# Two residue pairs at once in the last, single-batch filter group

## The chip, the cores and the metric

The kernel runs on one core of a Trainium2 chip. The metric is the device time of one execution in microseconds, the median over several runs. Five engines run their own instruction streams: TensorE (PE in the profile, with its weight loads as PEld), VectorE (DVE), ScalarE (ACT), GpSimd (POOL) and SyncE (SP), whose stream issues most of the DMA transfers.

## The reference

Two blocks follow each other for 8 batches of a 3008 x 256 array. The first filters along the sequence by a real FFT, a product with a complex filter and the inverse FFT; the second is an MLP mixer, first over the tokens, then over the channels.

```python
X = np.fft.rfft(x, axis=1)                       # x: (8, 3008, 256)
y = np.fft.irfft(X * (filt_r + 1j * filt_i), n=3008, axis=1)
h = np.maximum(y.transpose(0, 2, 1) @ w_tok1, 0.0) @ w_tok2     # 3008 -> 256 -> 3008
u = y + h.transpose(0, 2, 1)
out = u + np.maximum(u @ w_ch1, 0.0) @ w_ch2                    # 256 -> 1536 -> 256
```

## The kernel before

**The filter.** 3008 = 47 x 64. The transform is done as length-64 steps ("a" steps), then, for each of 32 residues k2, length-47 steps: forward (b), the product with the filter, and back (bi). The data between the a steps and the b steps goes through a DRAM tensor `z_tmp`, the filtered data through `g_tmp`, and the mixer reads it from there as `t4` tiles. The batches form five groups, `GROUPS = ((0,), (1, 2), (3, 4), (5, 6), (7,))`. The first two groups have code of their own. The last three are `tiled`: TensorE is used as four 64 x 64 tiles, and two residues (a pair, `KC = 2`) go through the length-47 step together. Groups (3, 4) and (5, 6) hold two batches of 256 columns side by side, so that their matmuls have 512 columns; group (7,) has `nb = 1` and 256.

For pair c of 16 in a tiled group:
- `b_pair(c)` (line 668): four tile matmuls through `four` (line 520), moving operand `t2` (loaded from `z_tmp`), weights from the table tile `wb`, into the two PSUM banks `acc` and `b`. Row tile h writes bank h, column tile i the partitions of half i. Every matmul of 32-bit floats is two passes, each with a weight load of its own.
- `products(c)` (line 673): for each bank one VectorE multiplication with the pair's filter tile, `filts[c % FB]` (`FB = 3`), to `p1` and `p2` (pools of one buffer each).
- `join(c)` (line 680): two VectorE operations that combine them in `p1`.
- `bi_pair(c)` (line 685): four tile matmuls, in pairs 0 to 14 to the two `pg` banks, which the mixer uses too, and for the last pair to `acc` and `b`; then two ScalarE copies (line 660) to `t3`, and two DMAs to `g_tmp`.

In program order, the step of pair c is b_pair(c), bi_pair(c - 1), products(c), the loads for pair c + 2 (four DMAs of `t2`, one of `wb`, eight of the filter by `filt_pair`, line 221), a yield, and join(c). All these loads and the stores to `g_tmp` are issued on SP's queue, in order. `turn` holds the two names `acc` and `b`; the mixer's `u_quarter` (line 856) and `token_product` (line 801) use the same two banks.

**The mixer.** `mix` (line 1054) runs over batches b, six m-tiles of the sequence, and `jp` of 0 to 5, six slices of the channel layer. One (b, m, jp) is called an item here, numbered i = 6m + jp, 0 to 35 in each batch. An item's order on TensorE is: `up_first` (line 944, four matmuls to the `pg` banks), `down` part 0 of the item before (line 978), `up_last` (line 960, three matmuls to the same `pg` banks), `down` parts 1 and 2. ScalarE copies a first sum `s`, VectorE makes `u2` (written to `hh`), two further columns of `s`, then `hh` (line 922), ScalarE applies the ReLU; VectorE's sums `t` of an item are used by `down` in the next. In some items `u_quarter` (lines 843 and 865) makes the next m-tile's input. At item 32 `token_product` makes the next batch's token layer in one run of matmuls (line 810), with VectorE sums `ts` ahead of each part.

**How the two are laid together.** The loop at line 1236 takes the mixer's yields one by one, and at each decides with the variable `coming` whether the filter generator `dft` of a coming group advances. The order is thus written by hand; no scheduler changes it. For a tiled group a b step goes between `down` parts 1 and 2 (place 1.5) of jp 1 and jp 4 (1 and 3 in the last m-tile), and a join one or two items later:

```python
due = (jp, place) in {"b": ((1, 1.5), (3 if tail else 4, 1.5)), "m": ((2, 2) if tail else (3, 1), (5, 1)),
                      "i": ((0, 1.5), (3 if tail else 4, 1.5))}[coming]
```

Group (7,) runs beside batches 5 and 6: its a steps in items 2 to 7 of batch 5, its b steps from item 10 of batch 5 to item 19 of batch 6, and its last bi_pair in item 22. The `t4` loads of batch 7 wait for its end (`next_ready`, line 1229).

Of the kernel before, what the change touches and what calls it, by code (L numbers as in the profile page):

```python
# [10 lines left out]
FP32 = mybir.dt.float32  # L11
# [3 lines left out]
ALU = mybir.AluOpType  # L15
# [7 lines left out]
D = 256  # L23
P = 128
# [3 lines left out]
KH = KR // 2  # L28
HALF = 64
# [3 lines left out]
FB = 3  # L33
XB = 2
XF = 2 * FB
KC = 2
# [91 lines left out]
def kernel(  # L128
# [11 lines left out]
    nc = tc.nc  # L140
# [7 lines left out]
    wbi_d = nc.inline_tensor(wbi_np, name="wbi_t").ap()  # L148
# [4 lines left out]
    place_of = {b: (g, i) for g, bs in enumerate(GROUPS) for i, b in enumerate(bs)}  # L153
    z_d, g_d = ([nc.dram_tensor("%s_tmp%d" % (what, g), shape + (len(bs), D), FP32, kind="Internal").ap()
                 for g, bs in enumerate(GROUPS)] for what, shape in (("z", (P, A)), ("g", (K2, KR))))
# [4 lines left out]
    def pool(name, bufs, **kw):  # L160
        return ctx.enter_context(tc.tile_pool(name=name, bufs=bufs, **kw))
# [4 lines left out]
    wbp = pool("wbp", 3)  # L166
    t2p = pool("t2p", 2)
    p1p = pool("p1p", 1)
    p2p = pool("p2p", 1)
    t3p = pool("t3p", 2)  # L170
# [11 lines left out]
    def bank(tag):  # L182
        return (psg if tag == "pg" else psum).tile([P, 512], FP32, tag=tag, name="ps_" + tag)
# [3 lines left out]
    turn = ["acc", "b"]  # L187
# [12 lines left out]
    filts = [glob.tile([P, 2, KC, D], FP32, name="filt%d" % i) for i in range(FB)]  # L200
# [319 lines left out]
    def four(outs, stat, mov):  # L520
        for i in range(2):
            for j in range(2):
                nc.tensor.matmul(outs(i, j), stat(i, j), mov(i, j), start=True, stop=True)  # L523

    def half_of(half, n=HALF):
        return slice(half * HALF, half * HALF + n)
# [30 lines left out]
    def dft(bs):  # L557
        first = bs[0] == 0
        nb = len(bs)
        tiled = bs not in GROUPS[0:2]  # L560
        todo = [(b, c) for b in bs for c in range(NXC // 2 if tiled else NXC)]
        wbs = {}
        kept = []

        def table_load(c):
            if first:
                if c < 5:
                    where, tag = (t1p, "t1") if c > 2 else (wbp, "wb")
                    t = where.tile([P, 2 * P, WC], FP32, tag=tag, name="wb")
                    for h in range(2):  # L570
                        nc.gpsimd.memset(t[half_of(h), ts(1 - h, P)], 0.0)
                    kept.append(t)
                wbs[c] = kept[c % 5]
                for h in range(2):
                    nc.sync.dma_start(wbs[c][half_of(h), ts(h, P)], wbi0_d[half_of(h), c])
            else:
                wbs[c] = wbp.tile([P, 4, HALF], FP32, tag="wb", name="wb")
                nc.sync.dma_start(wbs[c], wbi_d[:, c])

        def w_load(c):  # L580
            table_load(c)
            (filt_load if first else filt_pair)(c)
# [16 lines left out]
        for i, u in enumerate(todo):  # L599
# [14 lines left out]
            if first and (i + 1) % (NXC // 2) == 0:  # L614

                for d in range(i // (NXC // 2) * P, (i + 1) // (NXC // 2) * P, 16):
                    v = turned.rearrange("p s d -> p d s")[:, d:d + 16, :]
                    nc.vector.transpose(v, v)
        t2s, t3s, prods = {}, {}, {}

        def t2_load(c):
            if first:
                return
            t2s[c] = t2p.tile([P, KC, nb, D], FP32, tag="t2", name="t2")
            for h in range(2):
                z = z_d[place_of[bs[0]][0]].rearrange("(e h k) a b d -> e h a k b d", e=2, h=2)
                for e in range(2):
                    to = t2s[c][ds(h * HALF + e * A, A)]
                    k = c == 0
                    if k:  # L630
                        nc.sync.dma_start(to[:, 0:1], z[h, e, :, 0:1])
                    nc.sync.dma_start(to[:, k:KC], z[e, h, :, c * KC + k:c * KC + KC])
# [26 lines left out]
        def by_block(out, ps):  # L659
            nc.scalar.copy(out=out.rearrange("p b (e g i) -> p b g e i", e=DH, i=CW),  # L660
                           in_=ps.rearrange("p b (g e i) -> p b g e i", e=DH, i=CW))

        def two_banks(tags):
            return [bank(tag).rearrange("p (b d) -> p b d", b=2)[:, 0:nb, :] for tag in tags]

        def b_pair(c):
            pss, wb, t2 = two_banks(turn), wbs[c], t2s[c]
            four(lambda h, i: pss[h][half_of(i)], lambda h, i: wb[half_of(h, KH), i], lambda h, i: t2[half_of(h, KH), i])  # L670
            return pss

        def products(c, pss):
            where = (p1p, p2p)
            for h in range(2):
                prods[c, h] = where[h].tile([P, 2, nb, D], FP32, tag="p%d" % (h + 1), name="p%d" % (h + 1))
                nc.vector.tensor_tensor(out=prods[c, h], in0=pss[h].unsqueeze(1).to_broadcast([P, 2, nb, D]),
                                        in1=filts[c % FB][:, :, 0, :].unsqueeze(2).to_broadcast([P, 2, nb, D]), op=ALU.mult)

        def join(c):  # L680
            p1, p2 = prods[c, 0], prods.pop((c, 1))
            nc.vector.tensor_tensor(out=p1[:, 0], in0=p1[:, 0], in1=p2[:, 1], op=ALU.subtract)
            nc.vector.tensor_tensor(out=p1[:, 1], in0=p1[:, 1], in1=p2[:, 0], op=ALU.add)

        def bi_pair(c, tags):
            pss, wb, p = two_banks(tags), wbs[c], prods.pop((c, 0))
            four(lambda i, h: pss[i][half_of(h)], lambda i, h: wb[half_of(i), 2 + h], lambda i, h: p[half_of(i), h])
            t3 = t3p.tile([P, KC, nb, D], FP32, tag="t3", name="t3")
            for i in range(KC):
                by_block(t3[:, i], pss[i])  # L690
            for h in range(2):
                nc.sync.dma_start(g_d[place_of[bs[0]][0]][ts(c, KC), ts(h, KH)].rearrange("k r b d -> r k b d"),
                                    t3[half_of(h, KH)])

        for c in range(FB):
            if not first:
                nc.gpsimd.memset(filts[c][:, :, 0, :], 0.0)
        if not first:
            for c in range(2):
                w_load(c)  # L700
                t2_load(c)
        yield "w"
        yield "b"
        if not first:
            last = K2 // KC
            for c in range(last):
                pss = b_pair(c)
                if c and tiled:
                    bi_pair(c - 1, ("pg", "pg"))
                products(c, pss)  # L710
                if c + 2 < last:
                    t2_load(c + 2)
                    w_load(c + 2)
                yield "m"
                join(c)
                if not tiled or c + 1 == last:
                    yield "i"
                    bi_pair(c, turn)
                if c + 1 < last:
                    yield "b"  # L720
            return
        if first:
# [442 lines left out]
    with tc.manual_schedule():  # L1165
        nc.sync.dma_start(wa0, wa0_d)
        nc.vector.memset(turned[:, A:K2, :], 0.0)
        for t in filts:
            nc.vector.memset(t, 0.0)
        half = 0  # L1170
        second = dft(GROUPS[1])
        for i, _ in enumerate(dft(GROUPS[0])):
            if i == 0:
                nc.scalar.dma_start(wai_t, wait_d)
            k = i - NXC - 2

            if i < NXC:
                if i in (1, 3, 5, 7, 9):
                    start()
                if i == NXC - 1:  # L1180
                    copies()
                    for t, src in ((wa, wa_d), (was, was_d), (wai, wai_d), (ident, ident_d)):
                        nc.scalar.dma_start(t, src)
            elif k >= 0:
                if k == K2 - 5:
                    pause.append(True)
                while half < 2 * IN_B * (k + 1) // K2:
                    if half % 2:
                        convert_end()
                    else:  # L1190
                        convert_middle()
                    half += 1

                if 19 <= k < 25:
                    t4_load(0, k - 19, 0, PARTS[1])
                elif 26 <= k < 29:
                    for c in range(2):
                        t4_load(0, 2 * (k - 26) + c, PARTS[1], PARTS[2])
                elif k in (30, 31):
                    for c in range(3):  # L1200
                        t4_load(0, 3 * (k - 30) + c, PARTS[2], PARTS[3])
# [5 lines left out]
        both = wcp.tile([P, 2, JP, 7, P], FP32, tag="wc", name="wc")  # L1207
# [83 lines left out]
```

## Time and profile before

| What | Value |
|---|---|
| Median of 3 runs | 2424.17 us (2424.15 to 2425.02) |
| Profiled execution, its own time | 2425.85 us |
| Its span, first to last instruction | 2424.1 us |
| Mean granted TensorE clock | 0.995 |
| Items' starts on TensorE | 288, from 141.3 to 2405.2 us |
| Batch 5, items 0 to 35 (with the group's b steps) | 281.5 us |
| Batch 6 (with its other b steps) | 271.1 us |

The profile lists the busy time of each engine with its share of the span, then the chain of work that ended last, and groups of like instructions with their count, busy time and mean length. The timeline lists instructions by start, in us, merged while they are alike: start, length of the merged row, engine, line, operation, what it writes from what, tile size, shape, count. Matmuls overlap in the pipeline, so distances between their starts are read, not their lengths. A row `48*64 48x256` is a matmul on a tile of 48 rows and 64 columns with 256 moving columns; its two passes are counted one by one.

### The profile page before, as it was taken

The numbers are of one execution on the slowest core, as the hardware profiler recorded it, in microseconds if no ns is written. First come the engines' busy times: TensorE is split into PE (matmuls) and PEld (weight loads), VectorE is DVE, ScalarE is ACT, GpSimd is POOL, SyncE is SP. The second block draws the span as 40 slices with busy tenths as digits, with TensorE's granted clock in tenths as the row PEclk, the third lists the DMA queues.
The fourth block names the chain that finished last, engine by engine and source line by source line (L and its number), as shares of the span: only waits on it lengthen the run. The fifth ranks groups of instructions, "written<-read, shape, count | busy, mean of one in ns | idle before, by whom it ended". The sixth has DMA issues, their size and how long they took to land.

```text
span 2424.1 us, 35550 instructions
## 1 busy us (share of the span) xinstructions
PE 2382.0 (98%) x12340; PEld 1985.9 (82%) x12340; DVE 1942.6 (80%) x3684; ACT 686.5 (28%) x1355; POOL 619.6 (26%) x1115
## 2 busy tenths in 40 slices
PE   7999999999999999999999999999999999999998
PEld 4666676978888888987888888897889888898887
DVE  7798778787887888777888888877787788777776
ACT  5733322232222222123222222213221222222222
POOL 7476332113111211211121112112112112112121
PEclk8999999999999999999999999999999999999999
DMA  9975545544343322444344222434324221411100
GB/s 217 248 231 166 155 144 177 161 155 138 108 133 98 86 79 78 160 134 146 103 132 125 76 81 82 145 101 133 90 75 151 63 60 46 152 63 31 39 15 20
DMA packets 187420, 278.66 MB, mean 115 GB/s; under 512 B 35485, under 2 KB 125291, under 8 KB 187240
## 3 DMA queue, kind: packets, MB, share of 16 engines
q1 hardware_dynamic: 140952, 212.56, 29.1%
q0 software_dynamic: 34688, 53.83, 8.2%
q10 hardware_dynamic: 11600, 10.00, 1.3%
q8 instruction: 98, 1.61, 0.3%
q14 instruction: 82, 0.67, 0.1%
HBM read 193.52 MB, written 82.72 MB: 114 GB/s over the span
## 4 chain that ended last, share of the span: by engine, by line
PE 90%; DVE 4%; DMA 2%; ACT 1%; issue 1%; POOL 1%; SPq 0%; ACTq 0%; DVEq 0%; POOLq 0%
PE ps_po L978 33%; PE ps_pg L944 18%; PE ps_pg L960 14%; PE ps_b L523 4%; PE ps_b L810 3%; PE ps_acc L865 3%; PE ps_acc L810 2%; PE ps_b L865 2%; PE ps_b L843 2%; PE ps_acc L843 2%; PE ps_pg L523 1%; PE ps_b L759 1%; DVE t L922 1%; DVE hh L922 1%; DMA filt<-in_x_dram 1%
## 5 line engine op out<-in xcount | busy, mean ns | idle before, releaser
L1025 POOL DMA_DIRECT2D out_dram<-r x752 | 407.9, 550 | 1542.3 <-issue 1082.2
L922 DVE TENSOR_TENSOR hh<-ps_pg,s 128x512 f32<-128x512 f32 (+3 forms) x864 | 482.0, 585 | 184.3 <-ACT s L947 181.4
L965 ACT ACTIVATE hh<-hh 128x512 f32<-128x512 f32 (+1 forms) x576 | 347.7, 621 | 993.4 <-DVE hh L922 989.5
L978 PE MATMUL ps_po<-t,wc 128*128 128x256 f32 (+1 forms) x2304 | 553.5, 379 | 1.8 <-DVE t L922 1.8
L978 PEld LDWEIGHTS ps_po<-t,wc 128*128 128x128 f32 x2304 | 427.8, 190 | 122.6 <-issue 40.8
L978 PE MATMUL ps_po<-hh,wc 128*128 128x256 f32 (+1 forms) x1728 | 413.2, 375 | 1.0 <-POOL wc L382 0.8
L944 PE MATMUL ps_pg<-v,wc 128*128 128x256 f32 (+1 forms) x1728 | 413.3, 375 | 0.7 <-POOL wc L381 0.7
L944 PEld LDWEIGHTS ps_pg<-v,wc 128*128 128x128 f32 x1728 | 327.3, 190 | 41.3 <-DVE v L922 3.1
L978 PEld LDWEIGHTS ps_po<-hh,wc 128*128 128x128 f32 x1728 | 327.7, 190 | 39.6 <-POOL wc L382 2.0
L960 PE MATMUL ps_pg<-u,wc 128*128 128x256 f32 (+1 forms) x1152 | 292.9, 377 | 1.2 <-DVE hh L922 1.2
L922 DVE TENSOR_TENSOR t<-t,hh 128x256 f32<-128x256 f32 (+1 forms) x576 | 245.0, 425 | 19.8
L960 PEld LDWEIGHTS ps_pg<-u,wc 128*128 128x128 f32 x1152 | 216.7, 190 | 44.2 <-DVE hh L922 13.9
L922 DVE TENSOR_TENSOR s<-ps_pg,hh 128x512 f32<-128x512 f32 (+1 forms) x288 | 196.1, 681 | 30.0
L947 ACT COPY s<-ps_pg 128x256 f32<-128x256 f32 (+1 forms) x288 | 105.9, 368 | 362.7 <-PE ps_pg L944 360.5
L922 DVE TENSOR_TENSOR t<-hh 128x512 f32<-128x512 f32 (+1 forms) x288 | 195.0, 677 | 0.6 <-ACT hh L965 0.6
L944 PE MATMUL ps_pg<-u,wc 128*128 128x256 f32 (+1 forms) x576 | 169.3, 375 | 2.9 <-DVE hh L922 2.8
L960 PE MATMUL ps_pg<-v,wc 128*128 128x256 f32 (+1 forms) x576 | 168.8, 375 | 0.0
L944 PEld LDWEIGHTS ps_pg<-u,wc 128*128 128x128 f32 x576 | 108.1, 190 | 19.3 <-DVE hh L922 6.2
L922 DVE TENSOR_TENSOR u<-ps_acc,u 128x256 f32<-128x256 f32 (+1 forms) x84 | 46.2, 550 | 97.0 <-PE ps_acc L865 66.1
L960 PEld LDWEIGHTS ps_pg<-v,wc 128*128 128x128 f32 x576 | 109.1, 190 | 12.7
L922 DVE TENSOR_TENSOR u<-ps_b,u 128x512 f32<-128x512 f32 (+2 forms) x126 | 74.4, 591 | 28.9 <-PE ps_b L865 26.7
L865 PE MATMUL ps_acc<-w 128*128 128x256 f32 (+1 forms) x336 | 85.5, 377 | 1.0 <-ACT t L539 1.0
(152 smaller groups left out, 2661.9 us busy)
## 6 DMA issues: line engine op xcount, KB each, us to landing
w<-w_tmp SPq DMA_DIRECT2D x84, 448.0 KB
w<-w_tmp SPq DMA_DIRECT2D x35, 896.0 KB
out_dram<-r POOLq DMA_DIRECT2D x696, 32.0 KB, 2.5
t<-g_tmp SPq DMA_DIRECT2D x42, 512.0 KB
g_tmp<-t SPq DMA_DIRECT2D x96, 192.0 KB
t<-z_tmp SPq DMA_DIRECT2D x180, 96.0 KB
z_tmp<-t SPq DMA_DIRECT2D x60, 256.0 KB
filt<-in_x_dram SPq DMA_DIRECT2D x90, 128.0 KB
```

Source lines behind the costliest of these rows:

```text
L523: nc.tensor.matmul(outs(i, j), stat(i, j), mov(i, j), start=True, stop=True)
L759: nc.tensor.matmul(acc[:, t, :], w1[:, a, ts(t, P)], t4[b, a // TC4][:, a % TC4, :], start=(a == 0 and t == 0), stop=(a == A - 1 and t == ...
L810: nc.tensor.matmul(ps[:, at], w[:, n], mov, start=(j == 0 and i in (0, 2)), stop=(j == AP - 1 and i >= 5))
L843: nc.tensor.matmul(ps[:, ds(q * P, n)], t4[b, c][:, r, ts(dh, P)], wai[:, 0:n], start=(first and q == 0), stop=(not first and q == 3))
L865: nc.tensor.matmul(ps[:, ds(j * hw, hw)], h1[:, n, :], w2m[m % 2][:, at, 0:hw], start=(i < 2 and j == 0), stop=(j == len(todo) - 1))
L922: nc.vector.tensor_tensor(out=out, in0=in0, in1=in1, op=op)
L944: nc.tensor.matmul(ps[:, 0:hw], chan[0][:, jp, n, :], mov, start=True, stop=True)
L947: nc.scalar.copy(out=s[:, 0], in_=g[0][:, 0, 0:hw])
L960: nc.tensor.matmul(ps[:, 0:hw], chan[0][:, jp, n, :], mov, start=True, stop=True)
L965: nc.scalar.activation(out=hs, in_=hs, func=AF.Relu)
L978: nc.tensor.matmul(po[i][:, j, 0:hw], chan[1][:, jp, n, :], mov, start=(jp == 0 and first == 1), stop=(jp == JP - 1 and last == 1))
L1025: q.dma_start(bass.AP(tensor=ob.tensor, offset=ob.offset + row * D + g * cw, ap=[[N1 * D, 32], [D if h else -D, n], [1, cw]]), blocks[ts(g ...
```

## The change

In group (7,), two pairs of residues go through a step together (`per = 2`). For the groups with two batches, and the first two groups, `per` is 1 and nothing changes. Pair c and pair c + 1 stand side by side, 256 columns each, in each PSUM bank, and in `p1`, `p2`, `t2` and `t3`; the two table tiles are one. b_pair issues four tile matmuls for pair c and four for pair c + 1, bi_pair the same, so that a step has four sets of four in a row. Products become four multiplications (the two pairs have different filters), join stays at two, twice as wide. The eight double steps keep the places that the first eight steps have. The loads after a double step are those of `t2` for the pairs c + 4 and c + 5, and of the filters for c + 3 and c + 4, since there are only three filter tiles.

```diff
+        per = 2 // nb if tiled else 1
...
-                wbs[c] = wbp.tile([P, 4, HALF], FP32, tag="wb", name="wb")
-                nc.sync.dma_start(wbs[c], wbi_d[:, c])
+                if c % per == 0:
+                    both = wbp.tile([P, per, 4, HALF], FP32, tag="wb", name="wb")
+                    nc.sync.dma_start(both, wbi_d[:, c:c + per])
+                    wbs.update((c + j, both[:, j]) for j in range(per))
...
+        wide = per * nb
...
-            t2s[c] = t2p.tile([P, KC, nb, D], FP32, tag="t2", name="t2")
+            if c % per == 0:
+                both = t2p.tile([P, per, KC, nb, D], FP32, tag="t2", name="t2")
+                t2s.update((c + j, both[:, j]) for j in range(per))
...
+        def of(j):
+            return slice(j * nb, (j + 1) * nb)
...
         def b_pair(c):
-            pss, wb, t2 = two_banks(turn), wbs[c], t2s[c]
-            four(lambda h, i: pss[h][half_of(i)], lambda h, i: wb[half_of(h, KH), i], lambda h, i: t2[half_of(h, KH), i])
+            pss = two_banks(turn)
+            for j in range(per):
+                wb, t2 = wbs[c + j], t2s[c + j]
+                four(lambda h, i: pss[h][half_of(i), of(j)], lambda h, i: wb[half_of(h, KH), i],
+                     lambda h, i: t2[half_of(h, KH), i])
             return pss
...
-                prods[c, h] = where[h].tile([P, 2, nb, D], FP32, tag="p%d" % (h + 1), name="p%d" % (h + 1))
-                nc.vector.tensor_tensor(out=prods[c, h], in0=pss[h].unsqueeze(1).to_broadcast([P, 2, nb, D]),
-                                        in1=filts[c % FB][:, :, 0, :].unsqueeze(2).to_broadcast([P, 2, nb, D]), op=ALU.mult)
+                prods[c, h] = where[h].tile([P, 2, wide, D], FP32, tag="p%d" % (h + 1), name="p%d" % (h + 1))
+                for j in range(per):
+                    f = filts[(c + j) % FB][:, :, 0, :].unsqueeze(2).to_broadcast([P, 2, nb, D])
+                    nc.vector.tensor_tensor(out=prods[c, h][:, :, of(j)], in1=f, op=ALU.mult,
+                                            in0=pss[h][:, of(j)].unsqueeze(1).to_broadcast([P, 2, nb, D]))
...
         def bi_pair(c, tags):
-            pss, wb, p = two_banks(tags), wbs[c], prods.pop((c, 0))
-            four(lambda i, h: pss[i][half_of(h)], lambda i, h: wb[half_of(i), 2 + h], lambda i, h: p[half_of(i), h])
-            t3 = t3p.tile([P, KC, nb, D], FP32, tag="t3", name="t3")
-            for i in range(KC):
-                by_block(t3[:, i], pss[i])
+            pss, p = two_banks(tags), prods.pop((c, 0))
+            for j in range(per):
+                wb = wbs[c + j]
+                four(lambda i, h: pss[i][half_of(h), of(j)], lambda i, h: wb[half_of(i), 2 + h],
+                     lambda i, h: p[half_of(i), h, of(j)])
+            t3 = t3p.tile([P, per * KC, nb, D], FP32, tag="t3", name="t3")
...
+                for i in range(KC):
+                    by_block(t3[:, i::KC, 0], pss[i])
...
-            for c in range(last):
+            for c in range(0, last, per):
                 pss = b_pair(c)
                 if c and tiled:
-                    bi_pair(c - 1, ("pg", "pg"))
+                    bi_pair(c - per, ("pg", "pg"))
                 products(c, pss)
-                if c + 2 < last:
-                    t2_load(c + 2)
-                    w_load(c + 2)
+                for j in range(c + 2 * per, c + 3 * per):
+                    if j < last:
+                        t2_load(j)
+                for j in range(c + min(2 * per, FB), c + min(2 * per, FB) + per):
+                    if j < last:
+                        w_load(j)
                 yield "m"
                 join(c)
-                if not tiled or c + 1 == last:
+                if not tiled or c + per == last:
                     yield "i"
                     bi_pair(c, turn)
```

More of the change, by code (lines that the diff above doesn't have):

```diff
@@ L663, in two_banks @@
         def two_banks(tags):
-            return [bank(tag).rearrange("p (b d) -> p b d", b=2)[:, 0:nb, :] for tag in tags]
+            return [bank(tag).rearrange("p (b d) -> p b d", b=2)[:, 0:wide, :] for tag in tags]
+        def of(j):
+            return slice(j * nb, (j + 1) * nb)
         def b_pair(c):
-            pss, wb, t2 = two_banks(turn), wbs[c], t2s[c]
-            four(lambda h, i: pss[h][half_of(i)], lambda h, i: wb[half_of(h, KH), i], lambda h, i: t2[half_of(h, KH), i])
+            pss = two_banks(turn)
[3 more added lines that the diff above has]
+                     lambda h, i: t2[half_of(h, KH), i])
             return pss
@@ L685, in bi_pair @@
         def bi_pair(c, tags):
-            pss, wb, p = two_banks(tags), wbs[c], prods.pop((c, 0))
-            four(lambda i, h: pss[i][half_of(h)], lambda i, h: wb[half_of(i), 2 + h], lambda i, h: p[half_of(i), h])
-            t3 = t3p.tile([P, KC, nb, D], FP32, tag="t3", name="t3")
-            for i in range(KC):
-                by_block(t3[:, i], pss[i])
+            pss, p = two_banks(tags), prods.pop((c, 0))
[4 more added lines that the diff above has]
+            t3 = t3p.tile([P, per * KC, nb, D], FP32, tag="t3", name="t3")
+            if per == 1:
+                for i in range(KC):
+                    by_block(t3[:, i], pss[i])
+            else:
+                for i in range(KC):
+                    by_block(t3[:, i::KC, 0], pss[i])
             for h in range(2):
-                nc.sync.dma_start(g_d[place_of[bs[0]][0]][ts(c, KC), ts(h, KH)].rearrange("k r b d -> r k b d"),
+                nc.sync.dma_start(g_d[place_of[bs[0]][0]][ds(c * KC, per * KC), ts(h, KH)].rearrange("k r b d -> r k b d"),
                                     t3[half_of(h, KH)])
@@ L698, in dft @@
         if not first:
-            for c in range(2):
-                w_load(c)
+            for c in range(2 * per):
+                if c < FB:
+                    w_load(c)
                 t2_load(c)
@@ L705, in dft @@
             last = K2 // KC
-            for c in range(last):
+            for c in range(0, last, per):
                 pss = b_pair(c)
                 if c and tiled:
-                    bi_pair(c - 1, ("pg", "pg"))
+                    bi_pair(c - per, ("pg", "pg"))
                 products(c, pss)
-                if c + 2 < last:
-                    t2_load(c + 2)
-                    w_load(c + 2)
+                for j in range(c + 2 * per, c + 3 * per):
[4 more added lines that the diff above has]
+                        w_load(j)
                 yield "m"
                 join(c)
-                if not tiled or c + 1 == last:
+                if not tiled or c + per == last:
                     yield "i"
                     bi_pair(c, turn)
-                if c + 1 < last:
+                if c + per < last:
                     yield "b"
```

## The prediction

> **What bounds the kernel now.** I read the busy times first, then the chain that ended last, then TensorE's timeline around the changed steps.
>
> ```profile
> PE 2382.0 (98%) x12340; PEld 1985.9 (82%) x12340; DVE 1942.6 (80%) x3684; ACT 686.5 (28%) x1355; POOL 619.6 (26%) x1115
> PE 90%; DVE 4%; DMA 2%; ACT 1%; issue 1%; POOL 1%; SPq 0%; ACTq 0%; DVEq 0%; POOLq 0%
> ```
>
> The matrix unit is busy 98% of the span and is 90% of the chain: the program is one TensorE stream, and an edit counts by what it does to the time between two TensorE instructions. So I measure by item. An item (one jp of the mixer) begins where the line-944 matmuls `ps_pg<-u` start; the distance to the next such start is its length. From TensorE's timeline, a plain item of batch 7, where no filter step is left:
>
> ```profile
> 2202.37 0.59 PE L944 MATMUL ps_pg<-u,wc 128*128 128x256 f32 x2
> ...
> 2206.69 1.89 PE L978 MATMUL ps_po<-t,wc 128*128 128x256 f32 x8
> 2208.41 0.38 PE L944 MATMUL ps_pg<-u,wc 128*128 128x256 f32 x1
> ```
>
> 6.04 us. The same jp in batch 5 with a step of batch 7's filter in it (item 16: four tile matmuls of b_pair, four of bi_pair, two passes each, 256 wide):
>
> ```profile
> 1742.27 0.59 PE L944 MATMUL ps_pg<-u,wc 128*128 128x256 f32 x2
> ...
> 1746.59 1.03 PE L978 MATMUL ps_po<-t,wc 128*128 128x256 f32 x4
> 1747.54 0.43 PE L523 MATMUL ps_b<-t,wb 48*64 48x256 f32 x2
> 1747.56 0.43 PE L523 MATMUL ps_acc<-t,wb 48*64 48x256 f32 x2
> 1747.81 0.38 PE L523 MATMUL ps_b<-t,wb 48*64 48x256 f32 x2
> 1747.82 0.38 PE L523 MATMUL ps_acc<-t,wb 48*64 48x256 f32 x2
> 1748.02 0.61 PE L523 MATMUL ps_pg<-p,wb 64*64 64x256 f32 x8
> 1748.57 1.13 PE L978 MATMUL ps_po<-t,wc 128*128 128x256 f32 x4
> 1749.54 0.38 PE L944 MATMUL ps_pg<-u,wc 128*128 128x256 f32 x1
> ```
>
> 7.27 us, so the step costs 1.23. Four tiles run side by side as a wave, starting at 1747.54, .81, 1748.02 and about .24. The two-batch groups do the same step 512 wide (item 22 of batch 3):
>
> ```profile
> 1219.88 0.59 PE L944 MATMUL ps_pg<-u,wc 128*128 128x256 f32 x2
> ...
> 1225.15 0.65 PE L523 MATMUL ps_b<-t,wb 48*64 48x512 f32 x2
> ...
> 1227.03 1.13 PE L978 MATMUL ps_po<-t,wc 128*128 128x256 f32 x4
> 1228.00 0.38 PE L944 MATMUL ps_pg<-u,wc 128*128 128x256 f32 x1
> ```
>
> 8.12 us: 2.08 for double the columns. A step therefore has a price of its own. Two waves alone (item 10) cost 0.79 and four 1.23, which is 0.22 a wave and 0.35 fixed; 512 wide, two waves cost 1.22 and four 2.08, 0.43 a wave and 0.36 fixed.
>
> The steps at jp 1 show a second loss: 1.45 to 1.53 against 1.23 at jp 4. There bi_pair asks for the two ps_pg banks before VectorE has read hh out of them (waits of 1700 to 1902 us; then item 13):
>
> ```profile
> PEld ps_pg L523 <- DVE hh L922: 1.0, 4, 0.3
> 1723.63 0.84 PE L523 MATMUL ps_pg<-p,wb 64*64 64x256 f32 x8
> ```
>
> 0.84 for what takes 0.61 in item 16. The 512-wide steps at jp 1 cost 2.08 like those at jp 4: their b_pair runs 0.43 us longer and covers the wait.
>
> **What the Trainium skill says.** "TensorEngine Tiling (Array Packing)", Key Properties: a change of the tiling mode drains TensorE. The trace agrees: both borders of a step stand idle, 0.35 us together. "TensorE: Matmul & The Clock Gate", The mechanism: weight loads overlap running matmuls only where the row group differs. Here it doesn't hold: waves on the same four tiles start 0.21 to 0.22 apart though each loads new weights (131 ns). The tiling page, Instruction Overhead, gives some 60 cycles a matmul, an estimated 25 ns at the 2.4 GHz of the skill's NeuronCore Architecture section; a wave is four matmuls and four weight loads, 0.2 us if loads pay it too, just under 0.22. Its PSUM Bottleneck section warns that eviction gains nothing from tiling; here ScalarE pays 369 ns for 256 columns and 589 for 512.
>
> **The change, part by part.**
> Before, the 17 steps of batch 7's filter cost, item by item against a plain item of the same place: batch 5, items 10 to 33: 0.79 + 1.45 + 1.23 + 1.46 + 1.22 + 1.45 + 1.23 + 1.67 + 2.28 = 12.78; batch 6, items 1 to 22: 1.50 + 1.22 + 1.46 + 1.23 + 1.53 + 1.23 + 1.45 + 0.78 = 10.40. Together 23.18 us. No other item of batches 5 to 7 differs from plain by over 0.03, a-steps apart.
>
> After, there are eight double steps and one closing bi_pair, at items 10, 13, 16, 19, 22, 25, 28, 31 and 33 of batch 5, by TensorE's order. TensorE's 128 matmuls stay as they are.
> - Item 10 (b_pair alone, four waves): 0.35 + 4 x 0.22 = 1.22.
> - Items 13 to 28, eight waves each: 0.35 + 8 x 0.2175 = 2.09, six times: 12.54. The ps_pg wait is covered as in the 512-wide steps.
> - Item 31: 2.10 in batches 1 and 3; I take 2.11.
> - Item 32, token product: 0.15 and 0.28 longer in batches 3 and 1, because VectorE, behind with the products, is late with ts; 0.27 here.
> - Item 33: in batch 3 the join of 512 columns (0.69 + 0.70 against 0.41 + 0.42) puts TensorE 1.04 behind before the step begins; then a bi_pair of four waves, 1.23, into acc and b, free by then: 2.27.
> Sum 18.41, so 23.18 - 18.41 = **4.77 us less**. Eight fixed parts of 0.35 are 2.8 of it; the ps_pg waits, net of the tail, the rest.
>
> *VectorE*: products stay 32 of 128x512 (683 ns, starts 0.60 apart), now four in a row: 2.48 us where two of 128x1024 take 2.36. The 0.12 eats slack: s ends 1.1 us before line 960 needs it in item 25 of batch 3. They start when bi_pair ends, since p1 has one buffer, as before. Join: 32 of 256 (415) become 16 of 512 (about 696), 13.3 to 11.1 us. That 2.2 is under TensorE and worth nothing, except at item 33, where the longer pair stands ahead of u2, costed above.
> *ScalarE*: 32 copies of 369 become 16 of 589, also under TensorE. One double pair holds ps_pg for 1.07 us after the waves; line 944 wants the first bank 0.97 us after the first full matmul; the 512-wide steps have this and don't wait. If it did, some 0.1 us a step.
> *SP's queue*: 8 table loads and 16 g_tmp stores fewer. Per double step 2 stores, 8 t loads, 16 filt loads, perhaps one table: 27 issues for 15. Behind them queue the w2m and t4 loads, needed an m-tile (some 43 us) or more later, and the w1 loads of items 21 to 27, first needed at item 32; the token product's own w1 loads follow steps that load nothing more. Of the filters only one pair, the first 8, is due at the next step: from a step's start 3.3 us until the copy, 0.9 for stores, 8 x 0.40, 8 x 0.28 = 9.6, and landing. Nearest next step: 19.3 us. Nothing on the path. POOL has no change. Batch 7's t4 loads need not wait for item 22 of batch 6; nothing stood behind that.
> The unknown is a run of eight 256-wide waves, longer than any in the trace. From below: a wave under 0.2175 has no reason. From above: waves five to eight show their weight loads in full, 131 ns each. I take 0.2175, which waves three and four show.
>
> The profiled execution took 2425.85 us with a span of 2424.1; the median is 2424.17. The sum is in span, which I expect at 2419.3, and comes off the median equally: **2419.4**.
>
> **The rivals.**
> *Long runs don't stream.* The supply of instructions, or the weight loads, limits a run of 64 loads and passes. Item 16's four waves show none of it, but loads may have been fetched ahead for four and not for eight. Fully exposed: 7 steps x 4 waves x 0.131 = 3.7 us back, 2423.1; at half of it 2421.3. Chance 0.17.
> *More than the sum.* Item 33 without VectorE's delay (1.04), item 32 without its 0.27: 2418.1. Against it: batch 3 has both, with the same joins. Chance 0.08.
> *Late filters, slower.* Products of a double step need a pair loaded only one step ahead. If it lands after the step's 19 to 24 us, four products wait, VectorE being in order keeps u2 and s back, and TensorE stops. It decides from about 10 us of extra landing time. At 2 us a step over seven steps: 2424.17 - 4.77 + 14 = 2433.4. Against it, the SP sum; for it, that no view shows when an SP load lands. Chance 0.05.
> *That it does nothing* is excluded by the order: the nine steps are there.
>
> **How the numbers follow.** The sum has 0.70. Its own range: 0.03 either way on seven steps, 0.3 on item 33, 0.15 on item 32, half a microsecond of spread between runs: 2418.7 to 2420.2. About 0.2%, 4.85 us, is what a measurement of this kernel can tell from no change; the border, 2419.32, lies almost on the forecast, which gives 0.37 of the 0.70 to faster. With the second rival 0.45 faster; 0.33 and the first rival 0.50 the same; 0.05 slower. The range for 8 in 10 takes in the first rival up to some four fifths of its price, and the edge of the second: 2418.3 to 2422.4.
>
> **What would show it.** Right: items 13 to 28 of batch 5 at 8.13 us for jp 1 and 4 alike, ps_pg tile matmuls no longer waiting for hh, batch 6 plain from item 1, item 33 about 2.3 over plain. Wrong: waves in ps_pg more than 0.22 apart, or VectorE waiting on filt. The forecast falls if batches 5 and 6 together shrink by less than 4 us or more than 5.5.

## The result, and the profile after

The changed kernel takes 2420.86 us (median of 16 runs, 2417.71 to 2423.36) against 2424.68 us of the kernel before on the same chips; the ratio is 0.9981, with a 95% interval of 0.9975 to 0.9988. The ratio stands for 4.6 us less (2.9 to 6.1); the two medians lie 3.8 us apart. The profiled execution has a span of 2419.5 us. The busy times and the chain of its page:

```profile
PE 2373.8 (98%) x12340; PEld 1984.4 (82%) x12340; DVE 1943.4 (80%) x3668; ACT 686.2 (28%) x1339; POOL 622.8 (26%) x1115
PE 86%; DVE 6%; DMA 4%; issue 2%; POOL 1%; ACT 1%; SPq 0%; ACTq 0%; DVEq 0%; POOLq 0%
```

TensorE has the same 12340 instructions and is still busy 98% of the span; VectorE and ScalarE have 16 instructions fewer each. The chain's shares are no measure here: a second profiled execution of the same changed kernel gives TensorE 88%. The profiles of this study differ by some microseconds before batch 0, the first, is through (the start of batch 1 lies between 474.4 and 480.2 us), so everything below is read in items, which repeat to 0.03 us. Item 16 of batch 5 on TensorE's timeline (start, length of the merged row, engine, line, what it writes from what, tile, shape, count):

```profile
1743.57 0.59 PE L969 MATMUL ps_pg<-u,wc 128*128 128x256 f32 x2
...
1747.88 1.03 PE L1003 MATMUL ps_po<-t,wc 128*128 128x256 f32 x4
1748.84 0.43 PE L523 MATMUL ps_b<-t,wb 48*64 48x256 f32 x2
...
1749.11 0.38 PE L523 MATMUL ps_b<-t,wb 48*64 48x256 f32 x2
...
1749.33 0.38 PE L523 MATMUL ps_b<-t,wb 48*64 48x256 f32 x2
...
1749.54 0.38 PE L523 MATMUL ps_b<-t,wb 48*64 48x256 f32 x2
...
1749.76 1.05 PE L523 MATMUL ps_pg<-p,wb 64*64 64x256 f32 x16
1750.73 1.13 PE L1003 MATMUL ps_po<-t,wc 128*128 128x256 f32 x4
1751.70 0.59 PE L969 MATMUL ps_pg<-u,wc 128*128 128x256 f32 x2
```

Line 1003 is `down`, which was line 978, and line 969 is `up_first`. Four waves of b_pair start at 1748.84, 1749.11, .33 and .54, then bi_pair's four follow from 1749.76; the step's last 32 passes and loads stream as the first 32 did. The item is 8.13 us long (1743.57 to 1751.70) where it was 7.27, but it now does two pairs. The matmuls' own waits between 1700 and 1902 us (who waited for whom, total us, times, longest) are two short ones, both in item 33, and of the weight loads' waits (PEld) one lies at item 32:

```profile
PE ps_pg L985 <- DVE hh L947: 0.3, 1, 0.3
PE ps_po L1003 <- DVE t L947: 0.2, 1, 0.2
PEld ps_b L835 <- DVE ts L947: 0.3, 1, 0.3
```

No matmul or weight load of a step (line 523) waits for hh any more.

The steps of batch 7's filter, in us over a plain item of the same place:

| Items of batch 5 | Predicted | Measured |
|---|---|---|
| 10 (b_pair alone) | 1.22 | 1.22 |
| 13, 16, 19, 22, 25, 28, each | 2.09 | 2.09 |
| 31 | 2.11 | 2.11 |
| 32 (token product) | 0.27 | 0.28 |
| 33 (last bi_pair) | 2.27 | 2.25 |
| Batch 6, all items | 0 | 0 |

The sum is 18.4 us, as predicted, against 23.1 before (23.18 by the prediction's rounded terms). Batch 5 is 5.64 us longer than before (287.17 against 281.53) and batch 6 is 10.38 us shorter (260.67 against 271.05), 4.74 us less together. From the start of batch 1 to the start of the last item, the changed kernel takes 1923.8 us and the kernel before 1928.4.

### The profile page after: what moved, and what is told of

Read it like the earlier page. It is cut to its first block, busy times and chain, and to the rows that moved or that the text cites. A ratio compares the mean times of both kernels' runs of the same rounds, so it can differ in the third digit from the quotient of the medians.

```text
span 2419.5 us, 35455 instructions
## 1 busy us (share of the span) xinstructions
PE 2373.8 (98%) x12340; PEld 1984.4 (82%) x12340; DVE 1943.4 (80%) x3668; ACT 686.2 (28%) x1339; POOL 622.8 (26%) x1115
## 4 chain that ended last, share of the span: by engine, by line
PE 86%; DVE 6%; DMA 4%; issue 2%; POOL 1%; ACT 1%; SPq 0%; ACTq 0%; DVEq 0%; POOLq 0%
PE ps_po L1003 33%; PE ps_pg L969 18%; PE ps_pg L985 14%; PE ps_b L523 4%; PE ps_b L835 3%; PE ps_acc L890 3%; PE ps_acc L835 2%; PE ps_b L890 2%; PE ps_b L868 2%; PE ps_acc L868 2%; PE ps_pg L523 1%; DVE t L947 1%; DMA st<-in_moe_w_tok_dram 1%; DVE hh L947 1%; DMA filt<-in_x_dram 1%
```

## The experiments

The span from batch 1's start to the last item's start is used for sums, since it leaves the varying beginning out. Lines are those of each experiment's own kernel.

**Two changes of tiling more in a step (e1).** The question is whether the fixed 0.35 us belongs to the change of tiling or to the sets of four.

```diff
                 pss = b_pair(c)
+                if per == 2:
+                    yield "s"
                 if c and tiled:
                     bi_pair(c - per, ("pg", "pg"))
...
```

In the table of places, b_pair of this group moves from place 1.5 to place 1 (ahead of `down` part 1), and what follows the new yield keeps place 1.5.

> The changed kernel, with b_pair of each double step moved ahead of down part 1, and bi_pair left behind it, so that two ordinary matmuls stand between the two halves and TensorE changes its tiling twice more in each of the seven steps that have both. Matmuls, VectorE's and SP's orders stay. Theory (a fixed price of 0.35 us for each change to tiles and back, whatever the number of waves): items 13 to 31 of batch 5 go from 2.09 to about 2.44 over a plain item, 7 x 0.35 = 2.45 us more in all; item 10 stays at 1.23. Rival (the price belongs to each set of four, or to its waits, not to the change of tiling): within 0.1 us of the changed kernel.

Items 13 to 28 cost 2.44 us each and item 31 2.43; item 10 stays at 1.22. The sum is 2.5 us more (1926.3). Item 16 on TensorE's timeline:

```profile
1746.56 0.38 PE L523 MATMUL ps_b<-t,wb 48*64 48x256 f32 x2
...
1746.88 1.13 PE L1005 MATMUL ps_po<-t,wc 128*128 128x256 f32 x4
1747.94 1.09 PE L523 MATMUL ps_pg<-p,wb 64*64 64x256 f32 x16
1748.97 1.13 PE L1005 MATMUL ps_po<-t,wc 128*128 128x256 f32 x4
```

The last wave of b_pair starts at 1746.56, and the ordinary matmul comes 0.32 later where a further wave would come 0.22 later; four ordinary passes at 0.22 would end their turn at 1747.75, and the tiles resume at 1747.94. The rest of the 0.35 lies in the first wave, which is followed 0.27 later instead of 0.22. Same matmuls, same sets, one round trip more out of the tiling and back: 0.35 us in six of seven steps, 0.32 at item 31. The price belongs to the round trip, not to the sets.

What the time goes into is less clear. In item 16 of the changed kernel 0.09 us pass idle on the way in and 0.11 on the way out; the other 0.15 lie behind the first wave and the first full pass, which hold up the next one by 0.05 and 0.10 more than later ones do. The weight loads there (the bracket gives the idle time ahead; "issue" says that the profile shows nothing that was waited for):

```profile
1748.84 0.14 PEld L523 LDWEIGHTS ps_b<-t,wb 48*64 48x64 f32 x2 [0.33 <-issue]
1748.85 0.14 PEld L523 LDWEIGHTS ps_acc<-t,wb 48*64 48x64 f32 x2
1748.89 0.14 PEld L523 LDWEIGHTS ps_b<-t,wb 48*64 48x64 f32 x2
...
1750.73 0.30 PEld L1003 LDWEIGHTS ps_po<-t,wc 128*128 128x128 f32 x2 [0.39 <-issue]
```

At each border the first weight load starts only when its own matmul does, at 1748.84 and 1750.73, while the loads of the second wave start at 1748.89, 0.22 ahead of that wave. A drain of TensorE at the change of tiling, and a first weight load that nothing covers, are thus not told apart: no run here changes one without the other.

**bi_pair first (e2).** This takes the cover from the ps_pg banks.

```diff
-                pss = b_pair(c)
-                if c and tiled:
-                    bi_pair(c - per, ("pg", "pg"))
+                if per == 2:
+                    if c:
+                        bi_pair(c - per, ("pg", "pg"))
+                    pss = b_pair(c)
+                else:
+                    pss = b_pair(c)
+                    if c and tiled:
+                        bi_pair(c - per, ("pg", "pg"))
```

> The changed kernel, with bi_pair ahead of b_pair in each double step, so that the ps_pg banks are asked for at the start of the step. Theory (what the 256-wide steps lost at jp 1 was the wait for VectorE's last read of the ps_pg banks, and a long b_pair covers it): from the ends of hh and the starts of the steps in batch 3, 0.69 us more at items 13, 19 and 25, 0.9 at item 31, 0.25 at items 16, 22 and 28, about 3.7 us in all. Rival (the jp 1 loss came from something else, such as table or filter tiles): no change over 0.3 us.

Items 13, 19 and 25 cost 2.76 (0.67 more), item 31 2.98 (0.87 more), items 16, 22 and 28 2.32 (0.23 more); the 0.28 of item 32 is gone, which had not been expected. The sum is 3.3 us more. Item 32 is plain because TensorE is held up at item 31 and VectorE's products fall earlier against it: they start 1.14 us before item 32 does, instead of 0.72, and u2 is on time. The waits of this kernel, 1700 to 1902 us:

```profile
PEld ps_pg L523 <- DVE hh L952: 3.5, 8, 0.6
```

The weight loads of the ps_pg waves wait for VectorE's read of hh, eight times, where the changed kernel's list of the same stretch has no such row for line 523. The loss at jp 1 before the change was this wait, and half of a double step is long enough to hide it.

**Filters later (e3, then e9).** Against the rival of the late filters.

```diff
-                for j in range(c + min(2 * per, FB), c + min(2 * per, FB) + per):
-                    if j < last:
+                late = [j for j in range(c + min(2 * per, FB), c + min(2 * per, FB) + per) if j < last]
+                if per == 1:
+                    for j in late:
                         w_load(j)
                 yield "m"
                 join(c)
+                if per == 2:
+                    for j in late:
+                        nc.vector.memset(filts[j % FB][:, :, 0, 0:1], 0.0)
+                    for j in late:
+                        w_load(j)
```

This is e9; e3 lacks the two lines of the memset.

> The changed kernel, with the filter and table loads of a double step issued after its join, one or two items (7 to 15 us) later, so that they have 9 to 12 us left instead of 16 to 20. Theory (SP's loads have that much slack): batches 5 and 6 within 0.2 us of the changed kernel, no wait of VectorE's products for a filter tile. Rival of the late filters: if their landing takes as long as issue and 10 us more, each of six steps waits, 1 us or more a step, 6 us or more in all.

e3 says nothing of the rival: batch 5 is unchanged, but so are the loads. The first one after item 13's step starts 7.9 us after it in both kernels. SP runs ahead of the other engines, and a later place in the program holds it back only where it waits for something. e9 gives it something to wait for.

> The changed kernel; after each join in batch 7's group, VectorE writes one zero into each column pair of the two filter tiles that are loaded next, so that their loads can't be issued ahead of the join (in e3 they were: SP runs ahead of the other engines). After the jp 1 steps the first filter load then starts about 15.5 us after the step instead of 7.9, and some 8 us are left for eight issues of 0.28 us and the landing. Theory (the loads had that slack): batch 5 within 0.3 us of the changed kernel's. Rival of the late filters: VectorE's products wait for the tile after items 13, 19 and 25, and items 16, 22 and 28 grow by 1 us or more each.

The loads after the steps at jp 1 now start 17.5 us after the step (step at 1723.28, load at 1740.80), and the next step comes at 1748.31. Batch 5 takes 287.13 us, against 287.17 in the changed kernel. VectorE's waits before the products, 1700 to 1900 us:

```profile
DVE p L691 <- PE ps_pg L523: 1.5, 5, 0.5
DVE p L691 <- issue: 0.2, 1, 0.2
```

None is for a filter tile. The loads have over 9 us to spare at jp 1, where the pair that is needed next was issued some 5 us ahead of the next step and still came in time. After the steps at jp 4 the join follows sooner, and the first load starts 9.8 and 10.1 us after the step, at most 2.2 later than in the changed kernel; there the changed kernel leaves 8.3 us or more between the pair's last issue and the next step. The late filters did not happen, and at jp 1 they were not near.

**The join earlier (e4).** What holds item 33 back?

```diff
+                joins.append(c)
+                joined.append(join)
                 yield "m"
-                join(c)
+                run_joins()
...
+        run_joins()
         c = rp.tile([P, 8, P], FP32, tag="r", name="c")
```

A join now waits in a list. `token_product` runs it after its matmuls (the second cut); otherwise `dft` does, where it did before.

> The changed kernel, with the join that belongs to item 32 issued on VectorE ahead of the evictions of the token product (where VectorE stands idle for 2.4 us) instead of behind them; in batches 1, 3 and 5. Theory (at item 33 the join delays u2, s and t, and TensorE with them): item 33 goes from 3.25 to 2.10 over plain in batches 1 and 3 and from 2.25 to 1.22 in batch 5, 3.3 us less in all. Rival (the delay at item 33 is that of finish_h1 and the evictions): no change, or item 33 up to 0.3 us less.

Item 33 costs 2.08 us in batches 1 and 3 (3.25 in the changed kernel) and 1.22 in batch 5 (2.25): 3.4 us less in all (1920.4). VectorE's timeline at item 33 of batch 5, in the changed kernel:

```profile
1885.65 0.42 DVE L947 TENSOR_TENSOR c<-ps_b,c 128x256 f32<-128x256 f32 x1 [2.43 <-ACT c L841]
...
1886.85 0.68 DVE L696 TENSOR_TENSOR p<-p,p 128x512 f32<-128x512 f32 x1
1887.45 0.69 DVE L697 TENSOR_TENSOR p<-p,p 128x512 f32<-128x512 f32 x1
1888.05 0.39 DVE L947 TENSOR_TENSOR hh<-ps_pg,s 128x224 f32<-128x224 f32 x1
```

and with the join earlier:

```profile
1878.67 0.68 DVE L702 TENSOR_TENSOR p<-p,p 128x512 f32<-128x512 f32 x1
1879.27 0.69 DVE L703 TENSOR_TENSOR p<-p,p 128x512 f32<-128x512 f32 x1
1881.18 0.42 DVE L956 TENSOR_TENSOR c<-ps_b,c 128x256 f32<-128x256 f32 x1 [1.23 <-ACT c L850]
...
1882.38 0.38 DVE L956 TENSOR_TENSOR hh<-ps_pg,s 128x224 f32<-128x224 f32 x1
```

The brackets give the idle time ahead of an instruction. The join fits whole into VectorE's pause of 2.43 us, of which 1.23 are left, and u2 (the hh row) follows the evictions 1.20 us after their first instead of 2.40. Timed against the kernel before, this kernel has a ratio of 0.9960 (0.9947 to 0.9974).

> The kernel with the earlier join, timed: 3.4 us less than the changed kernel, about 0.33% under the kernel before.

Its median is 2416.63 us beside 2421.25 of the changed kernel on that chip, which was timed with it:

> The changed kernel itself, timed beside the two others on one chip: 4.7 us under the kernel before.

The changed kernel came to 0.9983 (0.9976 to 0.9989) there, 4.7 us by the medians. The earlier join stands 4.6 us under it by the medians, of five runs on one side; the items of the two profiles give 3.4, as in e4, and the rest lies in the part that varies.

**The step of item 31 moved to item 30 (e6).** In the table of places, jp `1` of the first b place became `0 if tail else 1`; the rest is e4.

> The kernel with the earlier join (e4), with the step of item 31 moved to item 30. Theory (the token product of item 32 starts late sums ts because VectorE is still behind with the products of item 31): item 32 falls back to within 0.03 us of plain, 0.7 us less in batches 1, 3 and 5 together, with 2.09 us at item 30 in place of 2.11 at 31. Rival (the 0.28 comes from the join ahead or from transfers of w1): item 32 stays at 0.14 to 0.28.

Item 32 is plain in batches 3 and 5, so there the products made it late. VectorE's timeline at item 32 of batch 5, which starts at 1860.94 in the changed kernel, shows them ahead of u2 (the hh row):

```profile
1860.22 1.29 DVE L691 TENSOR_TENSOR p<-ps_b,filt 128x512 f32<-128x512 f32 x2
1861.43 1.28 DVE L691 TENSOR_TENSOR p<-ps_acc,filt 128x512 f32<-128x512 f32 x2
1862.63 0.38 DVE L947 TENSOR_TENSOR hh<-ps_pg,s 128x224 f32<-128x224 f32 x1
```

u2 starts 1.68 us after the item does, where it starts at 1.39 in e6; the first ts is then about as late, and TensorE waits for it (the row of line 835 above). In batch 1 item 32 stays 0.28 over plain, and e5 and e7, which leave the step at 31, have 0.14 or 0.15 there. The products are not what adds to it: there ScalarE's first copy s is late. Its rows in batch 1 of the changed kernel, where the item starts at 719.96, and of e5, where it starts at 722.31:

```profile
721.25 0.35 ACT L972 COPY s<-ps_pg 128x224 f32<-128x224 f32 x1 [1.00 <-PE ps_pg L969]
...
723.33 0.34 ACT L991 COPY s<-ps_pg 128x224 f32<-128x224 f32 x1 [0.72 <-PE ps_pg L988]
```

In batch 1 the copy starts 1.29 us after the item's start in the kernel before, the changed kernel and e6, and 1.01 in e5 and e7; in batches 3 and 5 it starts at 1.01 in all of them. What holds it for 0.28 us, the profile doesn't show.

The move itself loses: e6 takes 4.8 us more than e4 in all, since item 31 now costs 1.73 to 1.86 us in each of the three batches, beside the 2.08 or 2.09 of item 30. VectorE is still at the products when the m-tile ends, and the waits show it at item 31 of batch 3 (TensorE's timeline, which gives the wait in brackets):

```profile
1290.06 1.40 PE L1012 MATMUL ps_po<-hh,wc 128*128 128x224 f32 x6 [0.53 <-DVE u L956]
1291.95 1.02 PE L994 MATMUL ps_pg<-u,wc 128*128 128x224 f32 x4 [0.49 <-DVE hh L956]
```

`down` of the next m-tile needs the po banks that VectorE's last sums of the old one (u) read, and those stand behind the products.

**The length-64 steps two at a time (e5, e7).** If each change of tiling has its price, the a steps pay it too. Both kernels have the earlier join of e4. The cut shows the loop, in which a double step's stores now share one t3 tile and one DMA.

```diff
-        for h in range(2):
-            z_out(b, pss[h], 2 * c + h, nc.sync)
+
+        def outs():
...
+            for i in range(0, len(todo), 2):
+                first_outs = a_pair(*todo[i], sds[0], turn)
+                last_outs = a_pair(*todo[i + 1], sds[1], ("pg", "pg"))
+                sds = [x_sums(*todo[j], j) for j in (i + 2, i + 3) if j < len(todo)]
+                more(2)
+                last_outs()
+                first_outs()
+                yield "a" if i + 2 < len(todo) else "w"
```

> The kernel with the earlier join (e4), in which also the length-64 steps of the three tiled groups go two at a time: eight tile matmuls in a row, into acc and b and then the two ps_pg banks, at place 1.5 of jp 1, 4 and 5, with ScalarE's copies into the idle t3 tiles. Six steps in batches 1 and 3 and three in batch 5 take the place of twelve and six. Theory (a step pays 0.35 us for its changes of tiling, and waves stream): each costs 0.35 + 4 x 0.43 = 2.09 us over a plain item, 12.5 us against 15.6 in batches 1 and 3 and 6.3 against 8.1 in batch 5: 8.1 us less in all than e4, a span of about 2406. Rival (VectorE's four sums, 2.5 us, or x tiles that are loaded only 8 us ahead hold the mixer up): 0.5 us or more lost in each of 15 steps, no gain over e4.

A double a step in a free place costs 2.08 us, where two single ones cost 2 x 1.22. But the sum is 1917.3, only 3.1 us less than e4, of 8.1 expected. Item 2 is 1.02 over plain without a step in it, since the first four sums stand on VectorE ahead of the mixer's u2, and item 7 costs 2.26 to 2.70. Besides, the expected sum took away the stalls of the old a steps at items 2, 3 and 9 (1.0 us a batch in 1 and 3), and the new stall at item 2 puts as much back.

> The kernel with the earlier join (e4) and the length-64 steps two at a time, now only at jp 1 and 4 of place 1.5, as the length-47 steps; a group's first x loads and sums start in the last two items of the batch before, so that batches 1 and 3 hold six such steps in items 1 to 16 and batch 5 three in items 1 to 7; the last bi_pair of the two-batch groups moves from item 28 to item 30. Theory (e5 lost its gain where VectorE's sums met the end of an m-tile at jp 5 and 0, and the two first sums in one go at item 1): the steps cost 2.09 us each, 2.3 at item 1; batches 1 and 3 fall by 2.9 us each against e4, batch 5 by 1.75, 7.5 us in all, about 2413 us beside 2424.5 of the kernel before. Rival (the first sums in items 35 and 0, or t4 loads that start two items later, hold TensorE up): less than half of that.

With the a steps at jp 1 and 4 alone, all cost 2.08 but the one of item 1, 2.96 to 2.97, where the sums of one x tile still meet the end of batch b - 1 on VectorE. The sum is 1915.1 us: 5.3 less than e4, of 7.5 expected. Item 1 alone makes up 2.0 of the missing 2.2: it was put at 2.3, in three batches. This is the fastest version: 2413.67 us, ratio 0.9949 (0.9936 to 0.9961) to the kernel before, 7.6 us under the changed kernel on the same chip.

## Why the prediction held

*The time.* The forecast was 2419.4 us and the measurement is 2420.86, inside the wide range but 1.5 us above the forecast and above the sum's own range, which ended at 2420.2. Of this 0.5 us is the kernel before, whose median is 2424.68 over 16 runs and was 2424.17 over three; the rest is that the medians lie 3.8 us apart, not 4.77, within the interval of the ratio. The time alone would fit the first rival at half its price (2421.3) better than the sum. That the sum was right, and the rival wrong, is shown by the items, and only by them.

*The price of a step.* The sum rested on 0.35 us for each change into the tiles and back, read from steps of two and four waves. e1 adds one such change to each of seven steps and finds 0.35 in six and 0.32 in the last. Eight of 17 went. The prediction's reading that both borders stand idle for the 0.35 is only in part so: 0.15 of it lie behind the first pass on either side. And where it says that the Trainium skill's page "TensorE: Matmul & The Clock Gate", The mechanism, doesn't hold here, it goes too far: the section also lets a weight load run ahead when it goes to the background weight buffer, which would fit waves that start 0.22 apart on the same tiles.

*The ps_pg wait.* The 0.23 us at jp 1 was put down to VectorE's last read of hh, hidden by a longer b_pair. e2 takes the cover away and finds the wait, 0.67 and 0.23 where 0.69 and 0.25 were worked out from the ends of hh (0.87 at item 31, of 0.9).

*Waves.* Eight 256-wide waves stream at 0.22 us; the first rival, exposed weight loads, is out: the step costs 2.09 and not 2.61.

*Items 32 and 33.* Costed from batches 1 and 3, to 0.02 us. The join's part is shown by e4. The part of the products in item 32 is shown by e6 for batches 3 and 5 alone. The prediction gave the products as the reason in batch 1 too, and there it is wrong: what is late is ScalarE's copy. That batch 1's 0.28 equals the 0.28 of batch 5 is chance; the 0.14 of batch 3 is the one with the same cause.

*SP's queue.* The conclusion held, its size didn't. The prediction gave the first filter pair 9.6 us from the step's start to its last issue. In the changed kernel it took 9.2 to 11.9 us, 10.4 after most steps, because the t loads took 0.48 us each, and up to 0.66, instead of 0.40. The longest is after item 16's step at 1748.84: eight t loads in 5.26 us, and the pair ended at 1760.74. The next step came at 1769.06 and was not touched; at jp 1, e9 shows that a last issue 20.0 us after the step would still do.

*The second rival* (item 33 without delay) was out by the forecast's own argument, and the delay is there. *The chances*: the reduction of 4.6 us is 0.19%, just on the near side of the 0.2% that the text took as its border, in the case that it gave 0.50. On which side of the border it fell is luck. As a limit of what can be measured the border was set too wide: with 16 runs the interval, 0.12% to 0.25%, leaves no change out.

## What to carry to other kernels

Where a kernel mixes small tiles with full matmuls, count the changes between them: here each round trip costs TensorE 0.35 us, with two, four or eight waves inside. In a stream that repeats to a few hundredths of a microsecond, the length of an item with and without a step, read off start times, forecasts better than any sum of busy times. And a place for more work is chosen by the other engines: 2.5 us of VectorE's sums or products are free at jp 1 and 4; where an m-tile ends, the products cost TensorE 1.7 to 1.9 us (e6).

## What the runs showed that was not expected

Moving DMA issues later in the program moved them by nothing (e3), since SP runs ahead to the next thing it must wait for. And TensorE's steady part repeats to 0.03 us an item from run to run and from chip to chip, while the part before batch 1 varies by almost 6 us over the profiles.
